# A decode-size forward and backward pass on one core: the FFN weights between the third and the last pass taken in turn, 512 units at a time

## The chip, the cores and the metric

One core of one Trainium2 chip runs the whole program in one launch. The metric is the device time of one execution in microseconds (us), from the first to the last instruction. The times given are medians of several executions.

The names of the engines in the profile: PE is the matrix engine (PEld is its loading of weights, which overlaps the matrix products), DVE the vector engine, ACT the scalar engine, POOL the general engine, SP the engine whose queue issues the loads.

## The reference: what is computed

The program computes the output and all gradients of four layers on a single token: attention over a cache of 65,536 positions, FFN, the same attention again, the same FFN again. Weights and caches are shared by the two halves.

```
x = A_x                                             # [1, 1, 1024]
x = x + attention(layernorm(x), k_cache, v_cache, wq, wo)   # 32 heads, 4 kv heads, 128 wide
x = x + ffn(layernorm(x), w1, b1, w2, b2)
x = x + attention(layernorm(x), ...same...)
x = x + ffn(layernorm(x), ...same...)

def ffn(n): h = n @ w1 + b1;  r = max(h, 0);  return (r * r) @ w2 + b2      # 1024 -> 3584 -> 1024
```

The reference returns the output and the gradients of the input, both caches, wq, wo, w1, b1, w2 and b2 for a given grad_out. In the text x1 to x4 are the values of x after the four lines, dx4 = grad_out, and dx3 to dx1 are the gradients at those points. The gradient of an FFN goes in two steps. First dh = 2 r * (w2 @ dx), which takes the dot products of the rows of w2 (one for each of 3,584 units) with dx. Then the gradient at the layer norm's output is w1 @ dh, which takes the rows of w1 (one for each of 1,024 inputs), or a sum over its columns. All caches and weights are in bf16.

## The kernel before, in words

**Passes and seams.** The two caches (64 MB each) don't fit on the chip, so they are streamed in four passes: forward through the first attention, forward through the second, backward through the second (pass 3, `attn_bwd3`), and backward through the first together with all gradients of the caches (pass 4, `attn_bwd4`). Between the passes lie seams, in which the FFNs are worked out. The seams are written as straight Python; the build's scheduler decides the order of the instructions on each engine there, while a pass has an order written out by hand or by stages. This case is about the seam between pass 3 and pass 4 (lines 1677 to 1714), which the code calls "dense34".

**The arena.** All large data lie in one arena of 20 slots of 1 MB (`Slot`, line 305; 128 partitions of 8 KB). Eight are planes that hold the softmax weights of both attentions until pass 4; of the other twelve, seven hold blocks of v that pass 3 kept for pass 4. Five slots rotate in the seam. `Slot` takes the free slot, and a load into it is issued on SP once the last instruction that used the slot is through. SP issues in order.

**What the seam does.**
1. The last of wq (`PRE["wq3"]`, two slots of 1 MB, loaded before the end of pass 3) is transposed in place, ahead of time. When pass 3 gives dqT, 64 products with it (line 701) give the last part of dn3. A layer norm's backward (`ln_bwd`, line 237) and an addition give dx2 (line 1686).
2. w2 goes past in seven blocks of 512 rows (`w2_slabs`, 1 MB each). `side_x4` (line 1699) multiplies each block with the activations of the second FFN, which gives x4 and so the output. The same block gives dh2, the row dots with dx2.
3. When all of dh2 is there, w1 goes past in eight blocks of 128 rows (`w1_slabs`, 896 KB each, rows of 7 KB). Its row dots with dh2 give the gradient at the layer norm, and `fin_dx1` makes dx1 of it (line 1693).
4. The first part of wo for pass 4 (two blocks of 1 MB) is transposed in place; 64 products with dx1 (line 701) give dO, with which pass 4 begins.

**Row dots.** The class `Rows` (line 592) works these out. A row dot over the free dimension can be made in two ways, and `front` (line 647) chooses by its own count of each engine's load. Either DVE multiplies the row with a broadcast copy of the vector and sums up (line 660, 1,024 elements at a time), or PE transposes eight 128 x 128 pieces (line 669), ACT or DVE brings the result from PSUM to a buffer `wt` (`evac`, lines 161 and 164; six such buffers), and `back` multiplies them with the vector (line 701, eight products of 64 equal columns). For the first way the vector must first be turned and broadcast to all partitions (`bcast_vec`, line 520: a transpose, one product for each 128 elements at line 531, casts). This happens once for dx2 (1,024 elements) and once for dh2 (3,584 elements, into a slot of its own). For transposes `Rows` uses three PSUM buffers `ps_tr` and two `ps_sc` in turn.

**x4.** After the last block of w2, `side_x4` adds bias and x3 (lines 1706 and 1707) and has x4 turned (line 205), cast (line 207) and stored (line 208).

Of the kernel before, what the change touches and what calls it, by code (L numbers as in the profile page):

```python
# [10 lines left out]
BF = mybir.dt.bfloat16  # L11
F32 = mybir.dt.float32
ACTF = mybir.ActivationFunctionType
ALU = mybir.AluOpType
AX = mybir.AxisListType
PSUM = bass.MemoryType.PSUM
P = 128
# [3 lines left out]
def kernel(  # L21
# [24 lines left out]
    nc = tc.nc  # L46
    D = A_x.shape[-1]
# [6 lines left out]
    F = B_w1.shape[1]  # L54
    DC, FC = D // P, F // P
# [19 lines left out]
    vec = ctx.enter_context(tc.tile_pool(name="vec", bufs=1))  # L75
    tmp = ctx.enter_context(tc.tile_pool(name="tmp", bufs=2))
# [11 lines left out]
    def ps_tr(shape=None, dtype=BF):  # L88
        return PS["pool"].tile(shape or [P, 8, P], dtype, name="ps_tr", tag="tr", bufs=2 if PS["pass4"] else 3)

    def ps_sc(shape, dtype=F32):
        return PS["pool"].tile(shape, dtype, name="ps_sc", tag="sc", bufs=1 if PS["pass4"] else 2)
# [4 lines left out]
    def ps_acc(shape):  # L97
        return PS["pool"].tile(shape, F32, name="ps_acc", tag="acc", bufs=1)
# [6 lines left out]
    def ps_bg(shape):  # L105
        return PS["pool"].tile(shape, F32, name="ps_bg", tag="bg", bufs=1)
# [4 lines left out]
    ident_b = const.tile([P, P], BF, name="ident_b")  # L111
# [33 lines left out]
    def add_load(act=0.0, dve=0.0, pe=0.0):  # L145
        load["act"] += act
        load["dve"] += dve
        load["pe"] += pe

    def evac(out, in_, kind="bf"):  # L150
        n = 1
        for d in in_.shape[1:]:
            n *= d
        ca = 0.17 + n * 0.00083
        cd = 0.13 + n * (0.00105 if kind == "f32" else 0.00054)

        if PS["pass4"] and kind == "bf":
            ca += 1.5
        if kind == "kta" or kind != "kt" and load["act"] + ca <= load["dve"] + cd:
            load["act"] += 0.17 + n * 0.00083  # L160
            nc.scalar.copy(out=out, in_=in_)  # L161
        else:
            load["dve"] += cd
            nc.vector.tensor_copy(out=out, in_=in_)  # L164
# [37 lines left out]
    def col_to_dram(col, n, v1d):  # L202
        nj = n // P
        pt = ps_mv([nj, P], F32)
        nc.tensor.transpose(pt[:, :], col[:, :], ident_f[:, :])  # L205
        rows = tmp.tile([nj, P], BF, name="rows_c", tag="rows_c")
        nc.vector.tensor_copy(out=rows[:], in_=pt[:])
        nc.gpsimd.dma_start(out=v1d.rearrange("(j p) -> j p", p=P), in_=rows[:])
# [28 lines left out]
    def ln_bwd(dn, n, rstd):  # L237
        st = tmp.tile([P, 2], F32, name="lnb_st")
        nc.vector.reduce_sum(out=st[:, 0:1], in_=dn, axis=AX.X)
        pr = tmp.tile([P, DC], F32, name="lnb_pr")  # L240
        nc.vector.tensor_tensor(out=pr[:], in0=dn, in1=n[:], op=ALU.mult)
        nc.vector.reduce_sum(out=st[:, 1:2], in_=pr[:], axis=AX.X)
        tot = bcast_sum(st[:], 2, mean=True)
        negm = tmp.tile([P, 2], F32, name="lnb_negm")
        nc.vector.tensor_scalar(out=negm[:], in0=tot[:], scalar1=-1.0, scalar2=None, op0=ALU.mult)
        t = tmp.tile([P, DC], F32, name="lnb_t")
        nc.vector.scalar_tensor_tensor(out=t[:], in0=n[:], scalar=negm[:, 1:2], in1=dn, op0=ALU.mult, op1=ALU.add)  # L247
        dx = tmp.tile([P, DC], F32, name="lnb_dx")
        nc.vector.tensor_scalar(out=dx[:], in0=t[:], scalar1=negm[:, 0:1], scalar2=rstd[:, 0:1], op0=ALU.add, op1=ALU.mult)  # L249
        return dx  # L250
# [172 lines left out]
    def d_cols(ap, nb):  # L423
        return ap[:, nb * P:(nb + 1) * P]

    def rows_of(W):
        return W.rearrange("(kc p) n -> p kc n", p=P)

    def f_rows_of(W):
        return W.rearrange("(s p j) n -> p s j n", p=P, j=4)  # L430
# [47 lines left out]
    def wo_slabs(g, ahead=1):  # L478
        v = rows_of(A_wo)
        return slabs("s_wo", lambda k, kn: v[:, g * R + k:g * R + k + kn, :], R, 4, 1024, ahead, True)  # L480
# [6 lines left out]
    def w1_slabs(ahead=1):  # L487
        v = rows_of(B_w1)
        return slabs("s_w1", lambda k, kn: v[:, k:k + kn, :], DC, 1, F, ahead)

    def w2_slabs(ahead=1):
        v = f_rows_of(B_w2)
        return slabs("s_w2", lambda k, kn: v[:, k // 4, :, :], FC, 4, D, ahead)
# [26 lines left out]
    def bcast_vec(vcol, nj, vbc=None, f=False):  # L520
        pt = ps_mv([nj, P], F32)
        nc.tensor.transpose(pt[:, :], vcol, ident_f[:, :])
        rows = tmp.tile([32, P], BF, name="bc_rows")
        nc.vector.tensor_copy(out=rows[0:nj, :], in_=pt[:, :])
        if vbc is None:
            vbc = mvs.tile([P, nj * P], BF, name="vbc", tag="vbc", bufs=1)
        for j0 in range(0, nj, 4):
            jn = min(4, nj - j0)
            pg = ps_gg() if PS["pass4"] else ps_tr([P, 512], F32)
            for jj in range(jn):  # L530
                nc.tensor.matmul(pg[:, jj * P:(jj + 1) * P], lhsT=ident_b[0:nj, j0 + jj:j0 + jj + 1].to_broadcast([nj, P]),
                                 rhs=rows[0:nj, :], start=True, stop=True)
            if f:
                evac(vbc[:, j0 * P:(j0 + jn) * P].rearrange("q (p j) -> q p j", j=4),
                     pg[:, 0:jn * P].rearrange("q (j p) -> q p j", j=4), kind="f32")
            else:
                evac(vbc[:, j0 * P:(j0 + jn) * P], pg[:, 0:jn * P], kind="f32")
        return vbc

    def to_cols_bf(vcol, nj):  # L540
        t = tmp.tile([P, 32], BF, name="vcb")
        nc.vector.tensor_copy(out=t[:, 0:nj], in_=vcol)
        return t
# [387 lines left out]
    def dO_finish(L, g):  # L931
        def fin(y):
            nc.vector.tensor_copy(out=L["dOT"][:, gsl(g)], in_=y)
            prod = tmp.tile([P, R], F32, name="dlt_prod")
            nc.vector.tensor_tensor(out=prod[:], in0=L["dOT"][:, gsl(g)], in1=L["oT"][:, gsl(g)], op=ALU.mult)
            yield
            pd = ps_mv([33, R], F32)
            nc.tensor.matmul(pd[:, :], lhsT=ones_f[:, 0:33], rhs=prod[:, :], start=True, stop=True)
            yield
            negd = tmp.tile([33, R], F32, name="negd")  # L940
            nc.vector.tensor_scalar(out=negd[:], in0=pd[:], scalar1=-1.0, scalar2=None, op0=ALU.mult)
            hi = tmp.tile([33, R], BF, name="negd_hi")
            nc.vector.tensor_copy(out=hi[:], in_=negd[:])
            lo = tmp.tile([33, R], BF, name="negd_lo")
            nc.vector.tensor_tensor(out=lo[:], in0=negd[:], in1=hi[:], op=ALU.subtract)
            nc.vector.tensor_copy(out=L["nd2"][0:1, gsl(g)], in_=hi[0:1, :])
            nc.vector.tensor_copy(out=L["nd2"][32:33, gsl(g)], in_=lo[32:33, :])
        return fin
# [736 lines left out]
        dxn3 = ln_bwd(dn3[:], L3["n"], L3["rstd"])  # L1685
        nc.vector.tensor_tensor(out=dx2[:], in0=dx3[:], in1=dxn3[:], op=ALU.add)

    def fin_dh2(y):
        nc.vector.scalar_tensor_tensor(out=dh2[:], in0=y, scalar=2.0, in1=L2["r"][:], op0=ALU.mult, op1=ALU.mult)

    def fin_dx1(y):
        dxn = ln_bwd(y, L2["n"], L2["rstd"])
        nc.vector.tensor_tensor(out=dx1[:], in0=dx2[:], in1=dxn[:], op=ALU.add)
    rows = Rows(DENSE["pool"])
    rows.add(PRE["wq3"], DC, R, lambda: L3["dqT"][:, gsl(lastg[2])], fin_dx2, inplace=True)
    x4 = vec.tile([P, DC], F32, name="x4")
    ps_x4 = ps_acc([P, DC, 64])

    def side_x4(kc, slab):
        for nb in range(DC):  # L1700
            nc.tensor.matmul(ps_x4[:, nb, :], lhsT=d_cols(slab, nb), rhs=L4["gb"][:, kc:kc + 1].to_broadcast([P, 64]),
                             start=kc == 0 and nb == 0, stop=kc == FC - 1 and nb == DC - 1, skip_group_check=True)
        add_load(pe=DC * 0.03)
        if kc == FC - 1:
            f = tmp.tile([P, DC], F32, name="ffn_f")
            nc.vector.tensor_tensor(out=f[:], in0=ps_x4[:, :, 0], in1=b2c[:], op=ALU.add)
            nc.vector.tensor_tensor(out=x4[:], in0=x3[:], in1=f[:], op=ALU.add)
            col_to_dram(x4, D, out_0.rearrange("a b d -> (a b d)"))
    rows.add(w2_slabs()[0], FC, DC, lambda: dx2[:], fin_dh2, mix=True, side=side_x4)
    rows.add(w1_slabs()[0], DC, FC, lambda: dh2[:], fin_dx1, cols=f_cols, mix=True)  # L1710
    rows.add(wo_slabs(firstg[3])[0], R, DC, lambda: dx1[:], dO_finish(L1, firstg[3]), inplace=True)
    rows.run()
    dst.close()
    psA_stack.close()
# [91 lines left out]
```

## Time and profile before

| | us |
|---|---|
| median of the three runs shown | 1986.36 |
| lowest and highest of them | 1979.23, 1986.77 |
| span of the profiled execution, first to last instruction (no other time of this execution is listed) | 1985.4 |
| PE busy in it | 1614.0 (81%) |
| DVE busy | 1174.4 (59%) |
| ACT busy | 1043.6 (53%) |
| read and written by DMA | 624.96 MB and 165.69 MB, 398 GB/s over the span |
| dx2 known (line 1686), from the span's start | 1165.1 |
| dx1 known (line 1693) | 1206.8 |
| last product of wo before pass 4 (line 701) | 1210.2 |

How to read the profile. The page divides the span into 40 equal slices of 49.6 us and gives for each the busy share of every engine, the busy share of the 16 DMA engines and the rate in GB/s. A query by stretches gives the same for any part of the span, with busy times in us and the number of instructions in brackets. A query in order of time lists instructions: start in us, duration in us, engine, line, operation, what is written and from what, the count of merged instructions, and in square brackets how long the engine stood idle before and who released it. The list of waits of SP says for which instruction a load's issue waited: total us, times, longest.

### The profile page before, as it was taken

What the parts mean: (1) busy time and instruction counts of PE and PEld (TensorE: products, weight loads), DVE (VectorE), ACT (ScalarE), POOL (GpSimd) and SP (SyncE); (2) the same over time, 40 slices, a digit from 0 to 9 for tenths busy, and PEclk for the clock granted to TensorE, in tenths of its full rate; (3) what the DMA queues carried; (4) which work ended last, traced back from release to release, by engine and by line L of the source; (5) the groups of instructions that cost most, each with busy time, mean ns of one, the idle gap of its engine ahead of it and who ended that gap; (6) DMA issues with size and microseconds to landing.
All of it is one profiled execution on the core that took longest, in us unless ns stands there. A gap on an engine that the chain in (4) does not pass through costs nothing. (4 is left out here: it accounts for less than half of the span.)

```text
span 1985.4 us, 67093 instructions
## 1 busy us (share of the span) xinstructions
PE 1614.0 (81%) x30228; PEld 1317.7 (66%) x30228; DVE 1174.4 (59%) x2426; ACT 1043.6 (53%) x1608; POOL 142.6 (7%) x332
## 2 busy tenths in 40 slices
PE   6878787687877877787877888887889898788897
PEld 6878777677777877786776886554556465455554
DVE  5645455255555543544544566877687586758666
ACT  3444344154344453534453455766678586657666
POOL 0000000000000000000000001111111111111211
PEclk9999899699999997998989999999899798879978
DMA  9999999999999998899999988999999999999996
GB/s 389 423 422 422 423 425 400 394 400 420 425 419 424 425 405 310 359 421 420 421 422 421 411 304 307 406 425 404 397 424 424 425 425 411 361 424 424 425 377 256
DMA packets 101037, 794.98 MB, mean 400 GB/s; under 512 B 9472, under 2 KB 9486, under 8 KB 37134
## 3 DMA queue, kind: packets, MB, share of 16 engines
q1 hardware_dynamic: 76670, 624.99, 76.6%
q0 software_dynamic: 24080, 165.70, 20.1%
q8 instruction: 236, 3.87, 0.8%
q14 instruction: 51, 0.42, 0.1%
HBM read 624.96 MB, written 165.69 MB: 398 GB/s over the span
## 5 line engine op out<-in xcount | busy, mean ns | idle before, releaser
L164 DVE COPY kt<-ps_tr 128x1024 bf16<-128x1024 bf16 x724 | 497.4, 689 | 431.0 <-PE ps_tr L1009 248.5
L161 ACT CAST arena<-ps_gg 128x1024 bf16<-128x1024 f32 x457 | 446.0, 1013 | 226.7 <-PE ps_gg L1393 140.2
L1009 PE MATMUL ps_tr<-ident_b,arena 128*128 128x128 bf16 x3840 | 310.4, 226 | 44.7 <-DMA arena<-in_A_k_cache_dram 30.7
L164 DVE CAST arena<-ps_gg 128x1024 bf16<-128x1024 f32 (+2 forms) x186 | 222.5, 1196 | 113.4 <-PE ps_gg L1471 47.8
L161 ACT COPY kt<-ps_tr 128x1024 bf16<-128x1024 bf16 x164 | 171.1, 1047 | 191.6 <-PE ps_tr L1201 111.7
L1009 PEld LDWEIGHTS <-arena 128*128 128x128 bf16 x3840 | 234.5, 101 | 54.0 <-DMA arena<-in_A_k_cache_dram 33.6
L1111 PE MATMUL ps_acc<-arena 128*128 128x64 bf16 (+4 forms) x4096 | 206.1, 196 | 66.1 <-DMA arena<-in_A_v_cache_dram 53.7
L1393 PE MATMUL ps_gg<-GG,xt 64*128 64x512 bf16 x1024 | 215.2, 418 | 28.2 <-ACT arena L161 10.1
L1111 PEld LDWEIGHTS <-arena 128*128 128x128 bf16 x4096 | 160.0, 101 | 71.8 <-DMA arena<-in_A_v_cache_dram 57.5
L1092 ACT ACTIVATE arena<-S_sb,L_negm 128x128 bf16<-128x128 f32 x256 | 165.6, 1003 | 61.1 <-DVE L_negm L1077 61.1
L1027 PE MATMUL ps_sc<-L_qpad,kt 128*128 128x64 bf16 (+7 forms) x3584 | 183.6, 194 | 11.2 <-issue 6.4
L1201 PE MATMUL ps_tr<-ident_b,arena 128*128 128x128 bf16 x1920 | 156.2, 227 | 44.4 <-DMA arena<-in_A_v_cache_dram 43.0
L1321 PE MATMUL ps_tr<-ident_b,arena 128*128 128x128 bf16 x1824 | 180.5, 235 | 10.4 <-DMA arena<-in_A_v_cache_dram 8.3
L1321 PEld LDWEIGHTS <-arena 128*128 128x128 bf16 x1824 | 118.9, 104 | 67.7 <-issue 56.9
L1027 PEld LDWEIGHTS <-kt 128*128 128x128 bf16 x3584 | 153.7, 100 | 15.2 <-issue 6.6
L1201 PEld LDWEIGHTS <-arena 128*128 128x128 bf16 x1920 | 118.6, 102 | 49.4 <-DMA arena<-in_A_v_cache_dram 45.5
L1424 PEld LDWEIGHTS <-arena 128*128 128x128 bf16 x2048 | 94.6, 102 | 59.8 <-issue 42.9
L1092 ACT ACTIVATION_READ_ACCUMULATOR arena<-S_sb,L_negm 128x1 f32 x256 | 128.1, 500 | 0.0
L1352 PEld LDWEIGHTS <-kt 128*128 128x128 bf16 x1824 | 84.5, 103 | 51.6 <-issue 50.1
L1352 PE MATMUL ps_sc<-DOB,kt 128*128 128x64 bf16 (+3 forms) x1824 | 114.7, 200 | 0.0
L1246 PE MATMUL ps_acc<-dsT,arena 128*128 128x64 bf16 (+7 forms) x2048 | 103.4, 194 | 13.5 <-DMA arena<-in_A_k_cache_dram 9.8
L1393 PEld LDWEIGHTS <-xt 64*128 64x128 bf16 x1024 | 65.7, 94 | 71.5 <-issue 33.0
(292 smaller groups left out, 2196.2 us busy)
## 6 DMA issues: line engine op xcount, KB each, us to landing
arena<-in_A_k_cache_dram SPq DMA_DIRECT2D x86, 2048.0 KB, 21.1
arena<-in_A_v_cache_dram SPq DMA_DIRECT2D x83, 2048.0 KB, 21.1
out_dram<-arena POOLq DMA_DIRECT2D x149, 1024.0 KB, 13.5
arena<-in_A_v_cache_dram SPq DMA_DIRECT2D x76, 1024.0 KB, 17.3
arena<-in_A_k_cache_dram SPq DMA_DIRECT2D x76, 1024.0 KB, 16.3
arena<-in_B_w_dram SPq DMA_DIRECT2D x32, 896.0 KB, 7.5
arena<-in_A_wo_dram SPq DMA_DIRECT2D x22, 1024.0 KB, 19.4
arena<-in_A_wq_dram SPq DMA_DIRECT2D x20, 1024.0 KB, 24.4
```

What stands on the lines that cost most here:

```text
L161: nc.scalar.copy(out=out, in_=in_)
L164: nc.vector.tensor_copy(out=out, in_=in_)
L1009: nc.tensor.transpose(pt[:, i, :], kb8[:, i, :], ident_b[:, :])
L1027: nc.tensor.matmul(state["ps_s"][:, s:s + w, :].rearrange("p a b -> p (a b)"), lhsT=kt[:, i, :], rhs=L["qpad"][:, g, 0:w, :].rearrange("p ...
L1092: nc.scalar.activation(out=E(p, g, c0, SU)[:, :, h], in_=S[:, h, :], func=ACTF.Exp, bias=L["negm"][:, g, su, h:h + 1], scale=SCALE, accum_ ...
L1111: nc.tensor.matmul(ps_o[:, 0:w, :], lhsT=vb8[:, i, :], rhs=E(p, g, c, w), start=(c % SU == 0), stop=(c % SU == SU - 1), skip_group_check=True)
L1201: nc.tensor.transpose(pt[:, i, :], vb8[:, i, :], ident_b[:, :])
L1246: nc.tensor.matmul(ps_dq[:, 0:w, :].rearrange("p a b -> p (a b)"), lhsT=kb8[:, i, :], rhs=dsT[:, s:s + w, :].rearrange("p a b -> p (a b)") ...
L1321: nc.tensor.transpose(pt[:, i, :], vb8[:, i, :], ident_b[:, :])
L1352: nc.tensor.matmul(state["ps_dp"][:, s:s + w, :].rearrange("p a b -> p (a b)"), lhsT=vt[:, i, :], rhs=DOB[:, g, 0:w, :].rearrange("p a b - ...
L1393: nc.tensor.matmul(pg[:, 512 * h:512 * h + 512], lhsT=xt[64 * h:64 * h + 64, j1 // 8 + m, :], rhs=gg[64 * h:64 * h + 64, :, :].rearrange(" ...
L1424: nc.tensor.matmul(ps_dq[:, 0:w, :].rearrange("p a b -> p (a b)"), lhsT=kb8[:, i, :], rhs=X[:, s:s + w, :].rearrange("p a b -> p (a b)"), ...
```

## The change

The last-but-one part of step 1 and steps 2 and 3 are written anew; `Rows` now only does wq and wo. w2 is still taken in blocks of 512 rows, but w1 is taken in blocks of 512 columns (all 1,024 rows, so that each load has 128 x 8 pieces of 1 KB). The blocks are loaded in turn: w2 slice 0, w1 slice 0, w2 slice 1, and so on, as far as there are free slots (`d_load`).

- `d_front(s)`: the products for x4 with w2 slice s; two of its four groups of 128 rows are transposed in place; w1 slice s is transposed into four buffers `wt` (now eight of them), and its slot is freed.
- `d_dh(s)`: the dots of w2 slice s with dx2, two groups by PE and two by DVE; the slot is freed; dh2 and its bf16 copy `dhb` for these 512 units.
- `d_bwd(s)`: 32 products of the transposed w1 slice with `dhb`, which are summed up over all slices in one PSUM tile.

The order in the program: wq's transposes, front 0, the products of wq, dx2, its broadcast, front 1, and then for each s: dh(s), bwd(s-1), front(s+1). The wo blocks, the last bwd, the layer norm's backward and dx1 follow, and then x4 is stored. dh2 is no longer broadcast. All transposes of fronts use the three `ps_tr` buffers.

```diff
-    rows.add(w2_slabs()[0], FC, DC, lambda: dx2[:], fin_dh2, mix=True, side=side_x4)
-    rows.add(w1_slabs()[0], DC, FC, lambda: dh2[:], fin_dx1, cols=f_cols, mix=True)
+    plan = deque(t + (s,) for s in range(NCH) for t in (("w2",), ("w1",)))
...
+    def d_load():
+        while plan and FREE:
+            t, s = plan.popleft()
+            sl = Slot("s_" + t)
+            if t == "w2":
+                v = sl.t[:, :].rearrange("p (k n) -> p k n", n=D)
+                nc.sync.dma_start(out=v, in_=f_rows_of(B_w2)[:, s, :, :])
+            else:
+                v = sl.t[:, :].rearrange("p (k n) -> p k n", n=512)
+                nc.sync.dma_start(out=v, in_=rows_of(B_w1)[:, :, 512 * s:512 * s + 512])
+            here[(t, s)] = (sl, v)
...
+    def d_front(s):
+        w2 = here[("w2", s)][1]
+        for j in range(4):
+            k = 4 * s + j
+            for nb in range(DC):
+                nc.tensor.matmul(ps_x4[:, nb, :], lhsT=d_cols(w2[:, j, :], nb), rhs=L4["gb"][:, k:k + 1].to_broadcast([P, 64]), ...)
+            if j < ON_PE:
+                pt = ps_tr()
+                for nb in range(DC):
+                    nc.tensor.transpose(pt[:, nb, :], d_cols(w2[:, j, :], nb), ident_b[:, :])
+                evac(w2[:, j, :], pt[:, :, :].rearrange("p a b -> p (a b)"))
+        w1 = here[("w1", s)][1]
+        for j in range(4):
+            pt = ps_tr()
+            for kc in range(DC):
+                nc.tensor.transpose(pt[:, kc, :], w1[:, kc, bass.ds(j, P, step=4)], ident_b[:, :])
+            wt = DENSE["pool"].tile([P, 8, P], BF, name="wt", tag="wt", bufs=8)
+            evac(wt[:, :, :], pt[:, :, :])
+            parts[(s, j)] = wt
+        d_free("w1", s)
...
+    def d_dh(s, dxb, dxbc):
+        w2 = here[("w2", s)][1]
+        ps = ps_sc([P, ON_PE, 64])
+        for j in range(ON_PE):
+            for nb in range(DC):
+                nc.tensor.matmul(ps[:, j, :], lhsT=d_cols(w2[:, j, :], nb), rhs=dxb[:, nb:nb + 1].to_broadcast([P, 64]), ...)
...
+        for j in range(ON_PE, 4):
+            nc.vector.scalar_tensor_tensor(out=junk[:, :], in0=w2[:, j, :], ..., in1=dxbc[:, :], ..., accum_out=y2[:, j:j + 1])
+        d_free("w2", s)
...
+    def d_bwd(s, ps):
+        for j in range(4):
+            wt = parts.pop((s, j))
+            for kc in range(DC):
+                nc.tensor.matmul(ps[:, kc, :], lhsT=wt[:, kc, :], rhs=dhb[:, 4 * s + j:4 * s + j + 1].to_broadcast([P, 64]), ...)
...
+    d_load()
+    rows.fill()
+    d_front(0)
+    rows.run()
+    d_load()
+    dxb = to_cols_bf(dx2[:], DC)
+    dhb = vec.tile([P, FC], BF, name="dhb")
+    dxbc = bcast_vec(dx2[:], DC)
+    d_front(1)
+    ps_dn = ps_bg([P, DC, 64])
+    for s in range(NCH):
+        d_dh(s, dxb, dxbc)
+        if s:
+            d_bwd(s - 1, ps_dn)
+        if 0 < s < NCH - 1:
+            d_front(s + 1)
...
     rows.add(wo_slabs(firstg[3])[0], R, DC, lambda: dx1[:], dO_finish(L1, firstg[3]), inplace=True)
+    rows.feed = None
+    rows.fill()
+    d_bwd(NCH - 1, ps_dn)
+    dxn2 = ln_bwd(ps_dn[:, :, 0], L2["n"], L2["rstd"])
+    nc.vector.tensor_tensor(out=dx1[:], in0=dx2[:], in1=dxn2[:], op=ALU.add)
+    col_to_dram(x4, D, out_0.rearrange("a b d -> (a b d)"))
     rows.run()
```

## The prediction

> **What bounds the kernel now.** I read the page's slices first, then the busy time by stretches around the third seam, then the instructions in order of time there, and last the waits of the DMA-issuing queue SP.
>
> ```profile
> DMA  9999999999999998899999988999999999999996
> GB/s 389 423 422 422 423 425 400 394 400 420 425 419 424 425 405 310 359 421 420 421 422 421 411 304 307 406 425 404 397 424 424 425 425 411 361 424 424 425 377 256
> ```
>
> In the four passes the DMA engines are full at 420 to 425 GB/s; there the kernel is bound by its 790 MB, and the change alters no byte. The holes are the seams. The one that the change touches lies in slices 24 and 25 (304 and 307 GB/s). By stretches of 10 us (columns: PE, PEld, DVE, ACT, POOL busy, then granted clock, DMA share, GB/s):
>
> ```profile
> 1150.00:1160.00 10.00, 7.04 (x150) 6.68 (x148) 1.92 (x6) 1.85 (x2) 0.00 (x0) 0.83 0.84 324
> 1160.00:1170.00 10.00, 9.71 (x237) 9.21 (x235) 6.93 (x22) 4.75 (x6) 0.00 (x0) 1.00 0.80 286
> 1170.00:1180.00 10.00, 8.56 (x225) 8.28 (x221) 10.00 (x19) 7.77 (x8) 0.00 (x0) 1.00 0.96 331
> 1180.00:1190.00 10.00, 9.05 (x175) 8.15 (x176) 6.26 (x19) 6.91 (x10) 1.16 (x11) 1.00 0.77 271
> 1190.00:1200.00 10.00, 8.84 (x195) 8.30 (x191) 8.53 (x17) 7.80 (x10) 0.00 (x0) 1.00 0.88 316
> 1200.00:1210.00 10.00, 8.12 (x165) 7.41 (x162) 7.00 (x21) 4.87 (x5) 0.61 (x1) 1.00 0.98 381
> 1210.00:1220.00 10.00, 8.22 (x148) 5.07 (x144) 7.20 (x35) 5.70 (x8) 2.38 (x6) 1.00 0.51 178
> ```
>
> From 1160 to 1210 PE is busy 44.3 of 50 us. The seam is long because PE, evictions and loads are all nearly full, not because one stands still. The instructions that carry the sums:
>
> ```profile
> 1146.28 1.06 PE L669 MATMUL ps_sc<-ident_b,arena 128*128 128x128 bf16 x16
> ...
> 1165.13 0.17 DVE L1686 TENSOR_TENSOR dx<-dx,lnb_dx 128x8 f32<-128x8 f32 x1
> ...
> 1168.35 0.41 PE L701 MATMUL ps_bg<-vcb,wt 128*128 128x64 bf16 x8
> ...
> 1169.55 0.66 PE L1701 MATMUL ps_acc<-L_gb,arena 128*128 128x64 bf16 x16
> ...
> 1180.95 0.27 PE L205 MATMUL ps_mv<-ident_f,x 128*8 128x128 f32 x1 [2.18 <-DVE x L1707]
> ...
> 1190.48 0.61 PE L669 MATMUL ps_tr<-ident_b,arena 128*128 128x128 bf16 x8
> ...
> 1208.01 2.15 PE L701 MATMUL ps_bg<-vcb,arena 128*128 128x64 bf16 x64
> ```
>
> Two dates frame the stage: dx2 at 1165.1 and the end of the last 64 products (wo) at 1210.2, after which the fourth pass begins; the DMA engines stand still from about 1208.4 to 1214, so a shift of 1210.2 shifts the end one for one. Prices on PE, from a run of 16 less a run of 8: a 64-wide product (0.66-0.41)/8 = 0.031 us, a transpose (1.06-0.61)/8 = 0.056 us.
>
> ```profile
> SPq L449 <- DVE mv_junk L660: 20.7, 9, 5.5
> SPq L449 <- PE ps_tr L669: 11.3, 3, 6.0
> ```
>
> The weight loads wait for slots that the row dots and transposes give back, so loads follow the compute. Five slots rotate here.
>
> **The change part by part.** *PE work.* By the order of instructions of the two kernels the stage's transposes go from 300 to 336, its products with a gradient from 300 to 336; the 224 products for x4 stay; 28 broadcast products of dh2 go (12 of them take 0.84 us and 8 take 0.60, so 0.06 each). Net 36 x 0.056 + 36 x 0.031 - 28 x 0.06 = +1.4 us. Nothing is saved on the fullest engine.
>
> *DVE and ACT.* Row dots of 1.15 us go from 17 whole and 3 half to 14, the seven casts of the dh2 broadcast (about 0.6 each) and the masks go, 40 evictions become 42, some 21 small operations of 0.18 come. DVE gets about 3 us lighter; it was not the last to end. A slice of 512 units costs DVE 2 x 1.15 + 2 x 0.69 + 3 x 0.19 = 4.3 us, ACT 4 x 1.0 = 4.0, PE 80 x 0.031 + 48 x 0.056 = 5.2.
>
> *Stalls that go.* PE's 2.2 us before L205, where x4 was turned in the middle of the stage (it now comes behind the last layer norm, and its cast of 0.28 lies on that chain); the dead end between dh2 and the w1 part (1184.9 to 1187.8), since each slice's gradient follows its own dots.
>
> *Loads.* w2 stays in rows of 8 KB: 128 packets on 16 engines at 309 ns (median of the trace's packet records) are 2.47 us. w1 was 8 blocks of 896 KB with 7 KB packets of 272 ns, 2.18 us each, 17.4 in all; it becomes 7 blocks of 1024 packets of 1 KB. Only 14 packets of 1 KB are in the trace (46 ns median): 64 x 46 ns = 2.94 us, 20.6 in all, +3.2 us. A slice is then 2.47 + 2.94 = 5.4 us of DMA beside 5.2 us of PE. What the trace doesn't show is how fast 1 KB packets can be issued. The nearest row is wq's 2 KB packets: 185 to 204 a us with the engines full. From below that gives 2.94 us (packets alone), from above 1024/195 = 5.25 us (no more packets a us than seen). I take 2.94, since at 195 a us the engines, not the issue, were the limit; both ends are kept.
>
> The Trainium skill (DMA: Bandwidth & Descriptors, Why small descriptors are slow) has three cycles on top of each packet's 32-byte beats. By that 1 KB would cost 35/32, some 8% over 8 KB, an estimate of 2.67 us a block; the 14 packets say 46 against 309/8 = 38.6 ns, 19%. The sum here uses the packets; by the page it would be 1.9 us of DMA less.
>
> *New waits.* A w2 block is now held from its landing until its row dots, which need dx2. So before dx2 only two slots come back from wq and one from the first w1 block, whose 32 transposes stand on PE between the wq products. Landings by packet records: second block 1156.7, third 1160.0; a block is used 2 to 3 us after its last packet (1198.35 to 1200.37, 1153.6 to 1156.6). So the first w1 block is usable near 1159.7, transposed by 1162.3, and dx2 keeps its 1165.1. Behind it: w1 slice 1 issued 1162.3, landed 1166.5, usable 1169, transposed 1171.5; only then its slot takes w2 slice 3, queued on SP behind w1 slice 3 (slot of w2 slice 0, whose row dots end near 1171 behind the vbc casts and two evictions). 2.94 + 2.47 us from 1172 land it at 1177.5, usable 1180. PE meanwhile has slices 1 and 2, and waits about 1.5 us at the first gradient product for its dhb; it is through near 1179.5. From 1180 four slices at 5.5 (the slower of PE and DMA, with some 0.1 for three transpose buffers in place of five) end at 1202.0. In the order of PE the 64 wo transposes (3.6) stand ahead of the last 32 gradient products (1.0): 1206.6. Layer norm to the cast of dx1: 1204.61 to 1207.17 before, 2.6, and 0.28 for x4's cast; then 2.15: 5.0. End **1211.6** against 1210.2: +1.4 us.
>
> The span is 1985.4; the median shown, 1986.36, is 1.0 above it, and I put the difference on the median: 1986.36 + 1.4 = **1987.8**.
>
> **The rivals.**
> *Fuller PE.* From dx2 on PE has 496 products (15.4), 288 transposes (16.1), 8 broadcasts (0.5), 64 wo transposes (3.6): 35.6 us. With no idle: 1165.4 + 35.6 + 5.0 = 1206.0, -4.2, **1982.2**. For it: the two stalls above are gone and DVE and ACT are lighter. Against: five slots and SP's order.
> *Same fill as now.* Before, the like sum is 29.6 us in the 38.1 from 1165.4 to 1203.5, 78%. 35.6/0.78 = 45.6: 1216.0, +5.9, **1992.2**. For it: transposes now have three buffers, and evictions sit behind row dots on DVE.
> *Slower: the issue of 1 KB packets.* At 5.25 us a block, from 1153.7 on seven w1 and six w2 blocks take 51.6, with 2 us of holes 1207.3, two wo blocks (2.65 each) 1212.6, usable 1214.8, half the wo transposes 1.8, products 1.0, tail 5.0: 1222.6, +12.4, **1998.8**. It decides once a w1 block takes over about 3 us, where DMA passes PE in each slice.
> *Faster by the pass's start.* If the idle of DMA at 1208 to 1214 closed as well: -4.2 - 6 = -10, **1976**. Against: that idle waits for the fourth pass's first products to free kept blocks, which follow the same date; the slots handed to that pass are the same in number and order.
> *No real change of order.* SP's order has w2 and w1 mixed (1, 1, 2, 3, 2, 1, then singly), so the change does what it says; what fails to come is a gain, as the forecast has it.
>
> **How the numbers follow.** Forecast 0.48, fuller PE 0.20, same fill 0.15, packet issue 0.12, pass's start 0.05. About 0.5% (9.9 us) is what a measurement of this kernel can tell from no change. The first three lie within it: 0.83; slower 0.12; faster 0.05. The range takes in the first three and the lower part of the fourth, and below the fuller PE the 3 us by which the runs shown scatter (down to 1979.2): 1979 to 1996.
>
> **What would show it.** Right: dx2 near 1165, PE's work from dx2 on near 35 us, w1 blocks landing about 3 us apart, the last wo product near 1211, the pass after it unchanged. Wrong: 1 KB packets far from 46 ns or with gaps between them, dx2 late because the first w1 block's transposes hold up the wq products on PE, or a seam under 40 us from dx2 to the last wo product. The forecast fails if either the slots or the packets set a slice at over 6.5 us or if the clock granted in the seam (0.83 in its first 10 us) changes.

## The result and the profile after

| | before | after |
|---|---|---|
| median of 14 runs each, us | 1983.35 | 1988.92 |
| lowest and highest | 1978.91, 1986.77 | 1984.92, 1991.51 |
| span of the profiled execution | 1985.4 | 1984.1 |
| stage: end of dx2 to the end of the last wo product | 44.86 | 48.77 |
| the same in a second profile of each | 45.88 | 50.48 |

The ratio of after to before is 1.0026, 95% interval 1.0018 to 1.0033. That is 5.2 us more (1983.35 x 0.0026), 3.6 to 6.5 by the interval. The forecast was 1.4 us more: the sign and the range hold, and the size is off by some 4 us. The single spans go the other way by 1.3 us. One profile can't carry such a difference; the stage inside it can, since both pairs of profiles have it longer, by 3.9 and 4.6 us.

The page of after, rate by slice:

```profile
GB/s 390 422 421 423 421 425 400 395 405 420 425 420 423 425 406 314 358 421 424 421 416 421 407 342 244 406 425 409 377 424 423 425 424 415 366 424 423 425 411 260
```

Slices 24 and 25, which had 304 and 307 GB/s, now have 342 and 244. Outside the seam no shift can be told from scatter: from the end of the last wo product to the end of the span it is 775.2 us before and 772.0 after, and 768.6 to 777.5 over all profiles of this study. By stretches of 10 us (same columns as before):

```profile
1170.00:1180.00 10.00, 8.44 (x194) 7.95 (x194) 7.99 (x21) 5.61 (x7) 0.00 (x0) 1.00 0.99 363
1180.00:1190.00 10.00, 9.14 (x207) 8.67 (x204) 8.18 (x18) 6.79 (x8) 0.00 (x0) 1.00 1.03 376
1190.00:1200.00 10.00, 8.53 (x192) 8.29 (x192) 5.36 (x16) 6.40 (x7) 0.00 (x0) 1.00 1.05 372
1200.00:1210.00 10.00, 7.33 (x156) 6.81 (x153) 5.67 (x18) 5.26 (x6) 0.96 (x2) 1.00 0.45 160
```

From 1170 to 1200 the queues are full (share 0.99 to 1.05; before 0.77 to 0.96), yet PE is busy only 8.4 to 9.1 of 10. What PE waited for there is in its instructions in order of time. In after, line 1718 is the product for x4, 1723 a transpose of w2, 1729 one of w1, 1760 the product with `dhb`, 669 a transpose of wo:

```profile
1178.26 0.42 PE L1718 MATMUL ps_acc<-L_gb,arena 128*128 128x64 bf16 x8 [0.27 <-DMA arena<-in_B_w_dram]
...
1188.19 1.17 PE L1760 MATMUL ps_bg<-dhb,wt 128*128 128x64 bf16 x32
...
1190.43 0.44 PE L1723 MATMUL ps_tr<-ident_b,arena 128*128 128x128 bf16 x5 [0.65 <-issue]
...
1195.54 0.33 PE L1723 MATMUL ps_tr<-ident_b,arena 128*128 128x128 bf16 x3
1196.91 0.44 PE L1723 MATMUL ps_tr<-ident_b,arena 128*128 128x128 bf16 x5 [1.05 <-issue]
...
1200.80 1.15 PE L1760 MATMUL ps_bg<-dhb,wt 128*128 128x64 bf16 x32
...
1203.12 1.33 PE L669 MATMUL ps_tr<-ident_b,arena 128*128 128x128 bf16 x21 [0.56 <-issue]
...
1206.08 1.16 PE L1760 MATMUL ps_bg<-dhb,wt 128*128 128x64 bf16 x32
...
1210.01 2.16 PE L701 MATMUL ps_bg<-vcb,arena 128*128 128x64 bf16 x64 [0.98 <-DVE vcb L542]
```

"issue" means that the profile shows nothing for which the engine waited. Here it stands in the middle of a run of eight transposes of one block: three are done, PE stands still for 1.05 us, five follow. No data can be missing between the third and the fourth. The slice before stops at the same place. Such stops take 2.45 us of the stage in this profile and 3.98 in the second. Before has none in its stage, in either profile, but it has them in other places. An example in the third pass, some 20 us ahead of the stage, is this stop between the sixth and the seventh of eight transposes:

```profile
1142.08 0.50 PE L1201 MATMUL ps_tr<-ident_b,arena 128*128 128x128 bf16 x6
1143.03 0.27 PE L1201 MATMUL ps_tr<-ident_b,arena 128*128 128x128 bf16 x2 [0.45 <-issue]
```

**What the stops are.** The page's list of queues has one for instructions:

```profile
q8 instruction: 236, 3.87, 0.8%
```

Its columns are packets, MB and share. All 236 packets have 16 KB. PE has 30,271 products and transposes and as many weight loads in this trace, 60,542 instructions; 60,542/236 = 257 a packet. So this queue brings PE's program, one packet for 256 instructions. One slice in after is 128 products and transposes (32 for x4, 16 and 32 transposes, 16 dots, 32 gradient products) and 128 weight loads: 256, one packet. In the packet records of after such packets begin at 1174.6, 1181.1, 1187.5, 1193.9 and 1200.4 (their clock is set against the instructions' by a constant, good to some tenths of a us), and the listed stops end at 1177.45, 1190.43, 1196.91 and 1203.12, 2.7 to 3.0 us after the first, third, fourth and fifth. (Where the second would show, a run of eight transposes takes 0.91 us in place of 0.61.) PE stands still for its next 256 instructions.

The whole traces bear this out. Count PE's products and weight loads through after, and all 54 of its "issue" stops (of 0.15 us and more, 41.8 us in all) stand at the same place of a block of 256, to within 14 instructions, and end 2.7 to 3.0 us after a packet's start. Before has 55 of them, 40.0 us in all (49 and 39.2 us in its second profile), at the same place. So such stops are not new with the change; what is new is that the stage has some. (What they cost in the passes, where the loads set the pace, was not tried.) The count also gives the borders at which no stop shows, and two times for each block: what PE needs from one border to the next (listed stops left out), and how long after a border the next packet begins (by the same constant).

| stage of | PE's time for a block, us | the next packet begins after the border, us |
|---|---|---|
| after, both profiles, the eight blocks that end in a listed stop | 5.4 to 6.1 | 3.4 to 4.3 |
| before, both profiles | 4.8 to 9.0 | at most 3.5, and at most 1.8 where PE's time is under 6 |
| ON_PE = 1 | 5.7 to 8.5 | 1.7 to 2.9 |
| parts of w1 and w2 | 5.3 to 9.0 | 0.1 to 2.8 |

(The last two are experiments below.) In these stages a packet begins about when PE passes a border or later, so PE has less than one block in hand. It stops where the packet's start and the 2.7 to 3.0 us behind it add up to more than its own time for the block: 3.4 to 4.3 and some 2.8 against 5.4 to 6.1 in after, at most 2.9 and 2.8 against 5.7 and more with ON_PE = 1.

That is what PE waits for; the experiments had to show what makes these loads late. "Stage" is below as in the table; PE's idle time in it is from its timeline (stops of 0.15 us and more):

| profile | stage | PE waits: own instructions | DVE and ACT | DMA | stage less own instructions |
|---|---|---|---|---|---|
| before | 44.86 | 0 | 3.85 | 1.59 | 44.9 |
| before, second | 45.88 | 0 | 3.34 | 2.16 | 45.9 |
| after | 48.77 | 2.45 | 4.29 | 0.27 | 46.3 |
| after, second | 50.48 | 3.98 | 4.29 | 0 | 46.5 |
| last products first | 48.11 | 4.19 | 2.51 | 0 | 43.9 |
| w1 in 8 KB rows | 51.66 | 3.64 | 4.29 | 0 | 48.0 |
| ON_PE = 1 | 44.91 | 0 | 7.05 | 0.71 | 44.9 |
| both of these edits (ON_PE, order) | 45.33 | 0 | 6.40 | 0.51 | 45.3 |
| before, x4 late | 46.35 | 0.66 | 1.93 | 3.16 | 45.7 |
| an eighth of w1 | 47.75 | 1.33 | 4.29 | 0 | 46.4 |
| parts of w1 and w2 | 45.25 | 0 | 3.53 | 0 | 45.3 |

### The profile page after: what moved, and what is told of

Its sections match the earlier page's. It is cut to its first block, busy times and chain, and to the rows that moved or that the text cites. A ratio compares the mean times of both kernels' runs of the same rounds, so it can differ in the third digit from the quotient of the medians.

```text
span 1984.1 us, 67134 instructions
## 1 busy us (share of the span) xinstructions
PE 1611.3 (81%) x30271; PEld 1314.3 (66%) x30271; DVE 1170.8 (59%) x2427; ACT 1039.1 (52%) x1601; POOL 141.5 (7%) x308
## 5 line engine op out<-in xcount | busy, mean ns | idle before, releaser
L1201 PEld LDWEIGHTS <-arena 128*128 128x128 bf16 x1920 | 119.5, 102 | 49.2 <-DMA arena<-in_A_v_cache_dram 46.5
L1424 PE MATMUL ps_acc<-X,arena 128*128 128x64 bf16 (+3 forms) x1536 | 101.0, 198 | 11.6 <-DMA arena<-in_A_k_cache_dram 11.6
```

The costliest lines, as they stand in the source:

```text
L1201: nc.tensor.transpose(pt[:, i, :], vb8[:, i, :], ident_b[:, :])
L1424: nc.tensor.matmul(ps_dq[:, 0:w, :].rearrange("p a b -> p (a b)"), lhsT=kb8[:, i, :], rhs=X[:, s:s + w, :].rearrange("p a b -> p (a b)"), ...
```

## The experiments

The first four ran beside 35 runs of before (median 1984.1), the next four beside 23 (1983.04), the last beside 15 (1985.22). Theory A: PE's work and its order set the stage. Theory B: the 1 KB packets set it. Theory C: PE's stops come from the many small packets. Later came D (the program's loads are late because the queues are full) and E (they are late because PE runs dense, whatever the queues do).

**The last 32 products ahead of wo's transposes.** Edit of after:

```diff
     rows.feed = None
-    rows.fill()
     d_bwd(NCH - 1, ps_dn)
```

> The changed kernel with the last 32 gradient products ahead of the 64 wo transposes on PE. The stage is measured from the end of dx2 (line 1686) to the end of the last 64 wo products: 44.9 us before, 48.8 after. Theory A (PE's work and its order set the stage; the wo transposes, 4.3 us in front of the last products, now lie on the path instead of beside the layer norm): the transposes go back beside the layer norm's chain, of which 2 us come off, 46.8, the time about 3.2 us above the kernel before. Theory B (the 1 KB packets of w1 set the stage): loads are as they were, 48.8, 5.2 us above.

Measured: 1986.49, ratio 1.0005 (0.9992 to 1.0018); stage 48.11. PE's waits in the stage (line, for what, us in total, times, longest):

```profile
PE ps_tr L1723 <- issue: 3.4, 3, 1.9
PE ps_bg L1760 <- issue: 0.8, 2, 0.6
PE ps_mv L212 <- DVE lnb_st L242: 0.3, 1, 0.3
```

Layer norm's wait at line 212 shrank from 0.88 to 0.32, since wo's transposes now fill it, and the stage less the stops is 43.9 against 46.4: 2.5 us for the order, which fits theory A (the stage itself, 48.11, isn't its 46.8). But the stops grew from 2.45 to 4.19 and took most of it back in this profile. The ratio, by 1.0005 against 1.0026, says about 4 us less than after, with intervals that just touch.

**w1's blocks in rows of 8 KB.** Edit of after; the data that lands is w2's, so the w1 part of the input gradient isn't computed:

```diff
-                nc.sync.dma_start(out=v, in_=rows_of(B_w1)[:, :, 512 * s:512 * s + 512])
+                nc.sync.dma_start(out=sl.t[:, :].rearrange("p (k n) -> p k n", n=D), in_=f_rows_of(B_w2)[:, s, :, :])
```

> The changed kernel, but each w1 block is loaded from the same slice of w2, in 128 rows of 8 KB instead of 1,024 pieces of 1 KB: the same bytes, slots and instructions, and w1 is left out of the computation. Theory A (PE's work and order): stage 48.8 as after, within 0.5. Theory B (1 KB packets): the landings of w1 blocks, 2.8 to 4.4 us apart, fall to 2.5, six of them after dx2, about 3 us: 45.8. Theory C (PE's stops for its own instructions, 2.5 us in after and none before, come from code loads queued behind the many small packets): those stops vanish, 46.3, while the loads' part stays.

Measured: 1985.74, ratio 1.0013 (1.0001 to 1.0025). PE's waits:

```profile
PE ps_tr L1723 <- issue: 2.5, 2, 2.0
...
PE ps_tr L669 <- issue: 1.1, 1, 1.1
```

The stops stay, 3.64 us with no 1 KB packet in the stage. So theory C falls. The stage didn't shrink either (51.66, of which the granted clock, 0.83 in 1190 to 1200 and in 1210 to 1220, explains a part), which speaks against B. The ratio is lower than after's by 0.0013, or 2.6 us, but the intervals overlap; what larger rows are worth here stays open.

**ON_PE = 1.** One of the two groups of w2 that PE transposes goes to DVE's row dots instead:

```diff
-    ON_PE = 2
+    ON_PE = 1
```

> The changed kernel with one of four groups of a w2 slice on PE instead of two, and three on DVE. After dx2 PE loses 48 transposes and 56 products, 48 x 0.056 + 56 x 0.031 = 4.4 us; DVE gains 7 x 1.15 = 8 us less some evictions and comes to 5.4 us a slice. Theory A: 3 us shorter, 45.8, the time 2 us above the kernel before. Theory B: DMA's 5.4 us a slice stay, 48.8. If DVE takes the place of PE: 49 or more.

Measured: 1982.92, ratio 0.9998 (0.9983 to 1.0013); stage 44.91. Stretches, and PE's waits:

```profile
1170.00:1180.00 10.00, 8.03 (x186) 7.67 (x184) 9.62 (x23) 7.17 (x8) 0.00 (x0) 1.00 1.01 377
1180.00:1190.00 10.00, 9.17 (x215) 8.77 (x212) 7.52 (x21) 8.77 (x11) 0.00 (x0) 1.00 1.00 351
1190.00:1200.00 10.00, 9.59 (x224) 9.39 (x221) 6.09 (x20) 7.78 (x10) 0.61 (x1) 1.00 1.05 396
```

```profile
PE ps_bg L1760 <- DVE dhb L1753: 1.9, 3, 1.3
PE ps_tr L1729 <- DVE wt L164: 1.2, 1, 1.2
PE ps_sc L1741 <- ACT arena L161: 1.0, 3, 0.5
```

Behind dx2 PE has 48 transposes and 56 dots less, 4.4 us by the prices of the prediction. In return it waits 2.8 us more for DVE and ACT (7.05 against 4.29), and its stops are gone, though the queues are as full as in after (1.00 to 1.05). A full queue alone doesn't make a stop: by the table of blocks PE needs 5.7 us and more for 256 instructions here, and the packets begin at most 2.9 us after a border.

**Kernel before, x4 taken out of the middle.** The diff's move of x4, alone, in the kernel before:

```diff
     def fin_dx1(y):
         dxn = ln_bwd(y, L2["n"], L2["rstd"])
         nc.vector.tensor_tensor(out=dx1[:], in0=dx2[:], in1=dxn[:], op=ALU.add)
+        f = tmp.tile([P, DC], F32, name="ffn_f")
+        nc.vector.tensor_tensor(out=f[:], in0=ps_x4[:, :, 0], in1=b2c[:], op=ALU.add)
+        nc.vector.tensor_tensor(out=x4[:], in0=x3[:], in1=f[:], op=ALU.add)
+        col_to_dram(x4, D, out_0.rearrange("a b d -> (a b d)"))
...
-        if kc == FC - 1:
-            f = tmp.tile([P, DC], F32, name="ffn_f")
-            nc.vector.tensor_tensor(out=f[:], in0=ps_x4[:, :, 0], in1=b2c[:], op=ALU.add)
-            nc.vector.tensor_tensor(out=x4[:], in0=x3[:], in1=f[:], op=ALU.add)
-            col_to_dram(x4, D, out_0.rearrange("a b d -> (a b d)"))
```

> The kernel before with one part of the change alone: x4's sum, its turning and store come behind dx1 instead of in the middle of the w2 part, where PE stood still 2.2 us for it. Theory A: PE's stop is on the path, the stage falls from 44.9 to 43, the time about 2 us below the kernel before. If the w2 loads or DVE set that part, the stage stays at 44.9 and the time is the same.

Measured: 1984.2, ratio 1.0000 (0.9985 to 1.0015); stage 46.35. PE's waits, first in this kernel, then in before:

```profile
PE ps_sc L669 <- DMA arena<-in_B_w_dram: 1.1, 1, 1.1
PE ps_sc L669 <- DMA arena<-in_A_wo_dram: 1.0, 1, 1.0
```

```profile
PE ps_mv L205 <- DVE x L1707: 2.2, 1, 2.2
```

The stop of 2.2 us is gone and nothing is won: the waits for loads double from 1.59 to 3.16. PE had been ahead of its loads, and the stop at x4 lay in that time. The stage also has one stop of 0.66 us for PE's own instructions, though it has the order of before: the block ahead of it takes PE 5.7 us, and the packet begins 3.5 us after the border.

**ON_PE = 1 and the last products first,** the two edits above together:

> The changed kernel with two edits together: ON_PE = 1 (one of the two transposed chunks of each slice's rows goes to the other engines instead of TensorE) and the last slice's products ahead of wo's transposes. Stage = from the end of dx2 to the end of the last wo product: 44.9 us in the kernel before, 48.8 in the changed one, 44.9 with ON_PE = 1 alone, 48.1 with the last products first alone. Theory A (TensorE's work, its order and its stops for its own instructions set the stage): the gains add, stage 43 to 45 us, ratio 0.998 to 1.000, so at or a little under the kernel before. Theory B (the loads of 1 KB rows set the stage): nothing over ON_PE = 1 alone, stage 44.9, ratio 1.000. If the stops for instructions return because TensorE runs denser: stage 46 to 48, ratio 1.001.

Measured: 1981.64, ratio 0.9995 (0.9984 to 1.0005); stage 45.33. The gains don't add. With ON_PE = 1 alone the stage was 44.91, so the second edit shows nothing in the stage once DVE is what PE waits for (4.76 us); a granted clock of 0.87 in 1180 to 1190, where it is 1.00 with ON_PE = 1 alone, may hide some of it. This is the best version of the study, and it can't be told from the kernel before.

**An eighth of each w1 block.** From the third slice on only the first 128 KB are loaded:

```diff
-                nc.sync.dma_start(out=v, in_=rows_of(B_w1)[:, :, 512 * s:512 * s + 512])
+                n = 8 if s < 2 else 1
+                nc.sync.dma_start(out=v[:, 0:n, :], in_=rows_of(B_w1)[:, 0:n, 512 * s:512 * s + 512])
```

> The changed kernel, but from the third slice on only an eighth of each w1 block is loaded (128 KB of 1 MB; the rest of the tile holds old data, so this part of the input gradient isn't computed). TensorE's work is the same. Tells whether TensorE's stops for its own instructions need full DMA queues. Theory D (the instruction load is late because it stands behind data in full queues): the stops (2.45 us in the changed kernel) fall under 0.7 us, stage 46.5 us or less, ratio at most 1.001. Theory E (the stops come from TensorE's density alone, 256 instructions a slice): the stops stay at 2 to 4 us, stage 48 to 49, ratio 1.002.

Measured: 1986.18, ratio 1.0018 (1.0007 to 1.0030); stage 47.75. Stretches and waits:

```profile
1180.00:1190.00 10.00, 9.50 (x232) 9.30 (x232) 9.00 (x23) 6.26 (x7) 0.00 (x0) 1.00 0.57 185
1190.00:1200.00 10.00, 9.50 (x230) 9.27 (x227) 4.34 (x12) 6.15 (x7) 0.00 (x0) 1.00 0.83 302
```

```profile
PE ps_tr L669 <- issue: 0.8, 1, 0.8
...
PE ps_tr L1724 <- issue: 0.5, 1, 0.5
```

Neither number is met: 1.33 us of stops lies between D's 0.7 and E's 2. Where they are tells more. From 1180 to 1190, at a DMA share of 0.57, there is none. The two end at 1194.72 and 1201.21; their packets begin at 1192.1 and 1198.4, in the stretch where the share is back at 0.83. So the queues had to be emptied further.

**Parts of w1 and w2.** As the last one, with w2's slices cut to a quarter from the third on:

```diff
-                nc.sync.dma_start(out=v, in_=f_rows_of(B_w2)[:, s, :, :])
+                n = 4 if s < 2 else 1
+                nc.sync.dma_start(out=v[:, 0:n, :], in_=f_rows_of(B_w2)[:, s, 0:n, :])
```

> As the run before it with an eighth of each w1 block, but w2 is cut too: from the third slice on only a quarter of each w2 slice (256 KB of 1 MB) and an eighth of each w1 block are loaded, so that the queues are nearly idle until wo's slabs; the rest of the tiles holds old data and these parts of the outputs aren't computed. TensorE's work is the same. With w1 alone cut the stops for instructions were 1.33 us and the stage 47.75, of which 46.4 without the stops. Theory D (the instruction load is late because it stands behind data in full queues): stops 0 to 0.3 us, stage 46.0 to 46.8, and the stage is TensorE's own work. Theory E (TensorE's density alone): stops of 1.3 us or more stay, stage 47.5 or more. If the loads rather than TensorE still set part of the stage, it falls under 45.5.

Measured: 1985.3, ratio 1.0000 (0.9988 to 1.0011); stage 45.25, no stop for instructions. Stretches, then PE in order of time at the place where after stopped for 1.05 us:

```profile
1180.00:1190.00 10.00, 9.25 (x218) 8.94 (x216) 10.00 (x22) 6.50 (x7) 0.00 (x0) 1.00 0.21 59
1190.00:1200.00 10.00, 9.80 (x232) 9.68 (x232) 4.97 (x15) 6.89 (x7) 0.00 (x0) 1.00 0.76 268
```

```profile
1194.24 1.15 PE L1762 MATMUL ps_bg<-dhb,wt 128*128 128x64 bf16 x32
...
1195.48 0.61 PE L1725 MATMUL ps_tr<-ident_b,arena 128*128 128x128 bf16 x8
```

The eight transposes run through in one piece (line 1725 here is 1723 in after). PE is denser than in after (9.80 of 10 us), so density alone doesn't make the stops, and E falls. D holds as far as it says that the loads make the packet late: by the table of blocks a packet begins at most 2.8 us after its border here, in after 3.4 to 4.3, while the packet itself takes about as long (0.93 to 1.13 us in this stage, 1.03 to 1.10 for the four of after's listed stops). What falls is the time until it moves. The stage is under the 46.0 that D gave, and under the 45.5 below which the loads set a part of it. They do, at its start: the second set of 32 products ends 11.9 us after dx2, in after 14.6. At the end a lower granted clock (0.67 in 1210 to 1220) took something back: the last 64 products need 3.32 us here, 2.16 in after.

**The two kernels once more,** one profile each:

> The kernel before, unchanged, for a second profile of the stage. If the stops for instructions belong to the change, none in the stage (under 0.5 us) and the stage at 44.9 us to within 0.7; if they come and go with the execution, 1 to 3 us of them here.

> The changed kernel, unchanged, for a second profile of the stage. If the stops for instructions belong to the change, 2 to 3 us of them again and the stage at 48.8 us to within 0.8; if they come and go with the execution, under 1 us of them and the stage near 46.5.

Before: stage 45.88, no such stop. After: stage 50.48, 0.9 us over the range expected, and 3.98 us of stops where 2 to 3 were:

```profile
1185.24 0.44 PE L1723 MATMUL ps_tr<-ident_b,arena 128*128 128x128 bf16 x5 [0.66 <-issue]
1192.28 0.44 PE L1723 MATMUL ps_tr<-ident_b,arena 128*128 128x128 bf16 x5 [1.20 <-issue]
1199.31 0.44 PE L1723 MATMUL ps_tr<-ident_b,arena 128*128 128x128 bf16 x5 [1.60 <-issue]
```

The place is the same, the length isn't: 0.65 and 1.05 in the first profile at the places that have 1.20 and 1.60 in this one. In this stage the stops came with the change in both profiles, and they vary in size. In both second profiles the clock fell inside the stage (0.86 granted in 1190 to 1200 in before, 0.66 in 1210 to 1220 in after), which lengthens both.

## Why the prediction was right in sign and small in size

- **The date of dx2** (kept at 1165.1): right. The transposes of the first w1 block don't hold up wq's products. dx2 ends 10.35 and 9.13 us after the third pass's last product, before 10.82 and 10.97.
- **1 KB packets** (46 ns, 2.94 us a block): right. In after 7,175 of them have a median of 46.0 and a mean of 50.0 ns, and from 1163 to 1168, where w1 has the load queue to itself, 330 to 380 of them begin in each us, 1,024 in some 2.9 us. So the cap of 195 in the slowest rival isn't there; that rival (+12.4) fell.
- **w2 slice 3 usable at 1180,** 14.9 us after dx2: right, 14.86 (1178.26, where PE waited 0.27 for it).
- **"four slices at 5.5": the step that failed.** From one set of gradient products to the next after takes 6.11 and 6.50 us (1188.19, 1194.30, 1200.80). Without the stops that lie in them, 0.65 and 1.05, it is 5.46 and 5.45. The work of a slice was priced to the tenth; that PE would stand still for its own program once in each slice was in no term, and the term was left at nothing without a reason: the trace of before, from which the prices came, has 55 such stops outside the stage. Over the stage they are 2.45 and 3.98 us.
- **wo's transposes ahead of the last products** (4.6 us): 5.45 from 1201.79 to 1207.24, of which 0.56 is a stop. The tail (5.0): 4.93 from there to 1212.17.
- **The stage:** predicted 46.5 (1165.1 to 1211.6). Measured, less the stops, 46.3, 46.5 and, with an eighth of w1, 46.4. With both profiles of each kernel the stage grew from a mean of 45.37 to one of 49.63, by 4.3 us: 3.2 of stops and 1.0 of what was predicted as 1.4. The medians' 5.2 has 4.3 within its 3.6 to 6.5.
- **"PE's 2.2 us before L205" goes:** it went, and was worth nothing. Moved alone, its time turned into waits for loads. The forecast, made of dates and not of a sum of stalls, hadn't counted it as a gain.
- **Rivals.** Fuller PE (-4.2) fell: PE waits 7.0 us in the stage of after (2.45 + 4.29 + 0.27), before 5.4. Same fill (+5.9) gave nearly the right time with the wrong cause: it put the loss on evictions and buffers, and PE's waits for evictions (`wt`, `arena`) are 2.0 us against 1.5. (The sums for DVE and ACT, 4.29 against 3.85 and 3.34, hide a swap: the wait at x4, 2.2 and 1.7, went, and 2.1 at the last layer norm came, which the forecast's tail of 5.0 holds.) The pass's start (-10) fell: the DMA share is 0.45 in 1200 to 1210, and the pass begins behind the last wo product as before.

The table of blocks also answers why the stage of before, with queues at 0.77 to 0.98, never stops, nor ON_PE = 1 with full ones. In before PE either takes 7 us and more for 256 instructions or has its packet early; with ON_PE = 1 its slice has 224 instructions in place of 256, so that a block lasts longer, and the packets begin earlier than in after.

What stays open: why a packet begins 3.4 to 4.3 us after the border in after and at most 2.9 with ON_PE = 1, at the same DMA share. The trace shows when a packet moves, not when it is asked for or behind what it stands. How much of the 5.2 us of the medians is stops rests on two profiles of each kernel.

## What to carry to other kernels

- Where a change makes PE the fullest engine while the DMA queues are full, PE's own program is a load like any other: count PE's instructions, weight loads too, and expect a stop where 256 of them take less time than the packet's start after the border and the 2.8 us behind it (5.7 to 7.1 us together in the full stages here). An "issue" wait in the middle of a run of equal instructions on one tile is its mark. Look for it in the whole trace of before: here it stood there 55 times, and a term for it could have been priced.
- A sum made of dates (which slot comes back when, what lands, when it is usable) held to 0.2 us over a stage of 46, once the stops were taken out; a list of stalls that go would have promised 2 us that weren't there.
- Taking work off the engine that is fullest (ON_PE = 1) shortened the stage more than the change of order did, until the next engine was what PE waited for.

## What was not expected of the hardware

- A PE program load under a full DMA: 16 KB packets of 1.05 us (median), and PE goes on 2.7 to 3.0 us after a packet's start. In these stages the packet for the next 256 instructions begins about when PE passes a border of 256 or later, up to 4.3 us later in after and 0.1 to 0.9 us with the queues at a share of 0.21 to 0.28. Stops of 0.19 to 2.02 us in the stages, 40.0 us in the whole span of before. The Trainium skill (Runtime: NRT & Kernel Launch, Instruction fetch mechanics) says that the program streams in blocks of 16 KiB, 256 instructions, and that crossing into the next is mostly hidden. The block agrees with this trace (257 instructions a packet). The second half doesn't hold here: 2.45 and 3.98 us of a stage of some 49 are not hidden, nor are 40.0 of 1985 in before.
- 1 KB packets take 46 ns where 8 KB take 309 (medians in after; means on the load queue 50.0 and 321), so per byte 19% more, 25% by the means. The page cited in the prediction gave 8%; 1,024 packets in some 2.9 us, not 2.67, side with the packet records.
